# A fused pre-norm attention and SwiGLU block on one core: 38 more of its transposes made by VectorE and a DRAM round trip, in a new list order

## The chip, the cores and the metric

One core of a Trainium2 chip. The metric is device microseconds per execution, the median of the runs. The profile is of one execution; its span goes from the first to the last instruction, and the execution's own time is a little longer. TensorE (PE) runs the matmuls, and in the profile its weight loads stand in a row of their own (PEld); VectorE is DVE, ScalarE is ACT, GpSimd is POOL; every DMA is issued on SyncE's queue (SP), in order.

## What is computed

A sequence of 2048 rows with 640 columns, in float32:

```python
h  = x + A(layernorm(x))        # A: qkv, attention over a window, times wo
h2 = h + B(layernorm(h))        # B: (silu(x @ w_gate) * (x @ w_up)) @ w_down
# A: 32 heads of 20; row s attends to rows s, s-2, ..., s-14 (8 keys, dilated by 2)
# wqkv 640 x 1920, wo 640 x 640, w_gate and w_up 640 x 1728, w_down 1728 x 640
```

## The kernel before

**Tiles.** The rows are cut into four blocks (b = 0 to 3) of 512 rows, each of four tiles j of 128 rows; the 32 heads into four head groups g of 160 columns. Matmuls run on fp32r operands that are split into a high and a low half (a copy by ScalarE, then a `tensor_sub` by VectorE), with three products for each: high times high, high times low, low times high. A block's normalised rows must be turned into columns for TensorE: 20 blocks of 128 x 128 (four row tiles, five column chunks). Their split columns lie in `sha` for blocks 0 and 2 and in `shb` for blocks 1 and 3; the columns of every block's second norm go to `shb` (to `ra` for block 3).

**Stages.** For every block: `load_x` and `ln1` (first norm, to columns), `qkv` for each head group (matmuls L546, evictions L551, DMAs of k, q and v to DRAM), attention of the head group on VectorE (L595 and L602 for the logits, L630 and L638 for the values), the output projection `wo` (L793) with the residual and the second norm, `ln2_columns`, then the FFN (`proj` L863, `down` L874). Blocks 2 and 3 share FFN products (L958, L980). TensorE has QKV and the transposes of block 1 to work on until wo(0), and QKV once more until the first FFN.

**Two ways to turn a norm into columns.** (1) On TensorE: four transposes by a 128 x 128 identity into a PSUM bank, then ScalarE copies the bank as the high half and VectorE subtracts for the low half (`to_columns`, L439, L442, L443; used by `x_columns`). (2) Through DRAM: ScalarE writes the centred or normalised rows sorted by 32 columns into `XN` (`LnStats.one` with `turned`, L300 to L304; `sorted_row`), VectorE turns all 32 x 32 blocks in one instruction (`turn_rows`, L412), four DMAs write to a DRAM tensor (L414 to `ysc`), one DMA reads it back into `XN` as columns (`turned_back`, L420), and ScalarE and VectorE split it (`turned_columns`, L428, L429). `turn_pair` (L381, L383, L387) and `pair_columns` (L395, L396, transposes L404) do that for the first two tiles of a block and leave ten transposes on TensorE for the other two; its DRAM tensor is `zsc`.

The attention's output has the same two ways. In `turned_out` VectorE turns a head group's output (L668) and four DMAs write it to `osc` (L672), from where `wo` loads it as columns. For a block in `TURNED`, the last head group stays in SBUF (`last_rows`, L644) and TensorE transposes it in `last_columns` (L733: per pair of tiles four transposes, one run).

Who goes which way stands at the top of the file (L28 to L30):

```python
TURNED = (0, 3)
HALF = (1, 2)
TURN1 = (2, 3)
```

`TURN1` are the blocks whose first norm goes through DRAM, `HALF` those of which half the second norm does, `TURNED` those whose last head group is transposed on TensorE. Block 1's first norm has its statistics on VectorE (`one_dve`, L347 to L349); block 0's first norm has code of its own in `ln1` (L507).

**The order of the work.** Every piece is added to a `Plan` with an engine, a cost in microseconds, the regions that it reads and writes, and a priority `PR[...]`; from the regions `add` makes its dependencies. `order` runs a list schedule over the engines with these costs: an engine that is free takes the ready piece of the lowest priority number. The start times found, plus hand-set offsets for a few pieces by number (`SHIFT`), are the keys by which all pieces are put into one list; the instructions are emitted in this order, so each engine's queue, SP's too, is a part of it. The semaphores follow from the regions and not from the modelled times.

Of the kernel before, what the change touches and what calls it, by code (L numbers as in the profile page):

```python
# [23 lines left out]
NF = 14  # L24
# [3 lines left out]
TURNED = (0, 3)  # L28
HALF = (1, 2)
TURN1 = (2, 3)  # L30
# [4 lines left out]
LAT, LAT0, RATE = 4.0, 2.0, 350e3  # L35
PR = {'x': 0.5, 'yst': 8, 'yld': 2, 'wqd': 4, 'wqh': 0.5, 'wql': 4, 'qev': 1, 'kvs': 0.4, 'atl': 1.2, 'exp': 0.5, 'ost': 3, 'wod': 2, 'woh': 8, 'wol': 1.2, 'old': 1.5, 'fld': 4, 'lst': 6, 'wev': 1.5, 'fh': 2.2, 'fl': 8, 'ln1': 8, 't1': 1, 'wo0': 1.2, 'wo': 2.2, 'ln1t': 1.2, 'xb': 0.4, 'tr': 10, 't1t': 2.2, 'ln1d': 0.5, 'hst': 10, 'hld': 10, 'ht': 1, 'hc': 2, 'jd': 3, 'jp': 8, 'js': 4, 'jl': 0.4, 'ja': 0.5, 'jfld': 1.2, 'jfh': 4, 'jfl': 1, 'jhi': 4, 'jmu': 0.4, 'jlo': 0.9, 'jcm': 0.5, 'w3': 1, 'w3e': 8, 'w3o': 0.4, 'w3x': 8, 'w3l': 2.2, 'jy': 6}

SHIFT = {
    10: 0.9, 12: 2.5, 34: 4.5, 47: -27.4, 113: 0.8, 131: -5.8, 2096: 10.8, 2101: 6.1, 2156: 4.1, 2712: 6.9,
    2713: 6.6, 2733: -78.6  # L40
# [3 lines left out]
class Plan:  # L44
# [23 lines left out]
    def order(self):  # L68
        ops = self.ops
        left = [len(o[3]) for o in ops]  # L70
        succ = [[] for _ in ops]
        for n, o in enumerate(ops):
            for d in o[3]:
                succ[d].append(n)
# [7 lines left out]
        bus, loaded, start = 0.0, None, [0.0] * len(ops)  # L82
        todo = len(ops)
        while todo:
            best = None
            for e in pend:
                if ready[e]:
                    t = free[e]
                elif pend[e]:
                    t = max(free[e], pend[e][0][0])  # L90
                else:
                    continue
                if best is None or t < best[0]:
                    best = (t, e)
            t, e = best
            while pend[e] and pend[e][0][0] <= t:
                m = heapq.heappop(pend[e])[1]
                heapq.heappush(ready[e], (ops[m][4], m))
            prio, n = ready[e][0]
            if e == "PE" and prio >= 10:  # L100
                soon = min((a for a, m in pend[e] if ops[m][4] == PR["wo0"]), default=1e9)
                if soon < t + 0.3:
                    free[e] = soon
                    continue
            if prio >= 20:
                soon = min((a for a, m in pend[e] if ops[m][4] <= 1), default=1e9)
                if soon < t + ops[n][1] - 0.3:
                    free[e] = soon
                    continue
            heapq.heappop(ready[e])  # L110
            todo -= 1
            _, cost, _, _, _, table, nbytes = ops[n]
            if table is not None and table != loaded:
                cost, loaded = cost + 1.3, table
            start[n] = t
            free[e] = t + cost
            end = t + cost
            if e == "SP":
                bus = max(bus, end) + nbytes / RATE
                free[e] = max(free[e], bus - 3.0)  # L120
                end = bus + (LAT0 if ops[n][4] == 0 else LAT)
            for m in succ[n]:
                same = ops[m][0] == e and e != "SP"
                avail[m] = max(avail[m], end + (0.0 if same else 0.2))
# [3 lines left out]
        self.end = max(free.values())  # L128
        self.start = start
        left = [len(o[3]) for o in ops]  # L130
        key = [(t + SHIFT.get(n, 0.0), n) for n, t in enumerate(start)]
        heap, out = [key[n] for n in range(len(ops)) if not left[n]], []
        heapq.heapify(heap)
        while heap:
            n = heapq.heappop(heap)[1]
            out.append(n)
            for m in succ[n]:
                left[m] -= 1
                if not left[m]:
                    heapq.heappush(heap, key[m])  # L140
        return out
# [9 lines left out]
def nb(chunks, size):  # L151
    return (chunks / 16 * 0.042 + chunks * size / 435e3) * RATE


def act(n):
    return 0.155 + 0.00087 * n


def program(tc, x_in, wqkv_in, wo_in, ffn_in, ffl_in, const_in, out):
# [7 lines left out]
    with tc.tile_pool(name="sb", bufs=1) as sb, tc.tile_pool(  # L167
# [106 lines left out]
        for nm, t in (("K", ksc), ("V", vsc)):  # L274
            P.add(
                "SP", 0.07, lambda t=t: zero_halo(t), r=[rf(PROD, 1120)],
                w=[(f"{nm}{g}{a}", 0, 7) for g in range(NG) for a in range(2)], prio=6, nbytes=36e3,
            )
# [111 lines left out]
        def pair_columns(b):  # L390
# [7 lines left out]
            for u, (n0, n) in enumerate(((10, 4), (14, 4), (18, 2))):  # L398
                bk = (7, 6, 5)[u]
                o, m = 128 * n0, 128 * n  # L400

                def tr(n0=n0, n=n, bk=bk):
                    for q in range(n):
                        T.transpose(banks[bk][:, 128 * q : 128 * q + 128], f(XN + 128 * (n0 + q), 128), ident)  # L404
                P.add("PE", 0.115 * n, tr, r=[rf(XN + o, m), rf(IDENT, 128)], w=[pb(bk)], prio=1)
# [30 lines left out]
        def to_columns(u, src, srcr, dst, dstr, bk, prio):  # L436
# [3 lines left out]
            P.add("PE", 0.46, tr, r=[srcr(4 * u + q) for q in range(4)] + [rf(IDENT, 128)], w=[pb(bk)], prio=prio)  # L440
# [32 lines left out]
        def ln1(b):  # L473
# [3 lines left out]
            st = LnStats(b, src, srcr, 1 if b == 0 else PR["ln1t" if b in TURN1 else "ln1"], rs=RS1 + 4 * b, center=True, turned=b in TURN1)  # L477
            if b:
                if b == 1:
                    st.prio = PR["ln1d"]  # L480
                    for j in range(NJ):
                        st.one_dve(j)
                else:
                    for j in range(NJ):
                        st.one(j)
                st.prio = 2
                st.rstd(0, NJ)
                if b in TURN1:
                    turn_rows(ysc, "Y", b, PR["tr"], PR["yst"])
                    return  # L490
                x_columns(
                    lambda u: (t()[:, 512 * u : 512 * u + 512], t()[:, 2560 + 512 * u : 3072 + 512 * u]),
                    lambda u: ((nm, 512 * u, 512 * u + 512), (nm, 2560 + 512 * u, 3072 + 512 * u)), PR["t1"])
                return
            for j in range(NJ):
# [3 lines left out]
                for c0, n, bk, bo in ((0, 4, 7 - j % 2, 0), (4, 1, 5, j)):  # L499
# [8 lines left out]
                    P.add("PE", 0.115 * n, tr, r=[rf(XN + x0, 128 * n), rf(IDENT, 128)], w=[key], prio=1)  # L508
# [17 lines left out]
        def qkv(b, g):  # L526
# [7 lines left out]
            for j in range(NJ):  # L534
# [12 lines left out]
                for ps in [[x] for x in whole] if b == g == 0 else [whole]:  # L547
                    P.add("PE", 0.218 * len(ps), lambda ps=ps, mm=mm: mm(ps),
# [157 lines left out]
        def last_columns(b, jp, at, sorted_, prio, rot):  # L706
# [27 lines left out]
            P.add("PE", 0.46, tr, r=[rf(last_rows(b, 2 * jp + jj), 160) for jj in range(2)] + [rf(IDENT, 128)], w=[pb(bk)], prio=prio)  # L734
# [6 lines left out]
        def wo(b, prio, bks):  # L741
# [25 lines left out]
            for j in range(NJ):  # L767
# [17 lines left out]
                for half in range(2):  # L785
# [8 lines left out]
                    P.add("PE", 2.25, mm, r=[rr(ot(5 * jp + i), 512) for i in range(5)] + [rr(WO, 6400)], w=[pb(bk)], prio=prio)  # L794
# [21 lines left out]
                if b in (0, 3) and j >= NJ - 2:  # L816
# [43 lines left out]
        def proj(bk, gu, col, wid):  # L860
# [3 lines left out]
            for p, (w, a) in enumerate(((0, 0), (0, 1), (1, 0))):  # L864
                P.add("PE", 1.145, lambda p=p, w=w, a=a: mm(p, w, a), r=[rr(gu + 1280 * w, wid * NC), ("shb", 2560 * a, 2560 * a + 2560)], w=[pb(bk)], prio=10)
# [13 lines left out]
        def downs(batch, first, last, db=DB, cut=False, whole=False):  # L879

            for k in (4, 0, 1, 2, 3):
# [8 lines left out]
                P.add("PE", sum(3 if t[0] < NF - 1 else 2 for t in batch) * 0.229,  # L890
# [61 lines left out]
        def product(bk, terms, start, stop):  # L952

            for p, (w, a) in enumerate(((0, 0), (0, 1), (1, 0))):
# [6 lines left out]
                P.add("PE", 0.229 * n, mm, r=[z for ws, _, cs, xr in terms for z in [rr(ws[w], 256 * len(cs) - 128)] + xr(a)], w=[pb(bk)], prio=10)  # L961
# [7 lines left out]
        def plain(i, x, xr):  # L969
# [6 lines left out]
            for bk, col in ((5, 0), (6, 128))[: 2 if i < NF - 1 else 1]:  # L976
                for p, (w, a) in enumerate(((0, 0), (0, 1), (1, 0))):
# [3 lines left out]
                    P.add("PE", 1.145, mm, r=[rr(gu + 1280 * w, wid * NC)] + xr(a), w=[pb(bk)], prio=10)  # L981
# [171 lines left out]
        def finish(b, db=DB, store=True, final=False):  # L1153
# [7 lines left out]
            P.add("PE", 0.46, tr, r=[rf(so, 512), rf(IDENT, 128)], w=[pb(d4)], prio=0)  # L1161
# [49 lines left out]
        for b, g in first + last:  # L1211
            if g == 0 and b > 0:
# [116 lines left out]
```

## Time and profile before

| | |
|---|---|
| median of 3 runs | 844.8 us (844.69 to 845.16) |
| the profiled execution | 845.0 us, span 843.0 us, granted TensorE clock 1.000 |
| VectorE, busy in the span | 705.1 us (84%) |
| ScalarE, busy in the span | 406.5 us (48%) |
| DMA | 191.12 MB, mean 227 GB/s |

A line of the page's groups or of its chain names the source line (L546 is line 546 of the kernel), engine, operation and tiles, `out<-in`. A row of the timeline begins with the start and the length in microseconds, and ends with the number of instructions merged into it; a bracket behind it tells how long the engine was idle before and which instruction ended that. Matmuls overlap by their pipelining, so a merged row is a little longer than the distance to the next row. A row of the waits says who waited for whom: microseconds in total, times, longest. A row of the DMA issues ends with the count, the size of each and the median time from issue to landing.

### The profile page before, as it was taken

The numbers are of one execution on the slowest core, as the hardware profiler recorded it, in microseconds if no ns is written. First come the engines' busy times: TensorE is split into PE (matmuls) and PEld (weight loads), VectorE is DVE, ScalarE is ACT, GpSimd is POOL, SyncE is SP. The second block draws the span as 40 slices with busy tenths as digits, with TensorE's granted clock in tenths as the row PEclk, the third lists the DMA queues.
The fourth block names the chain that finished last, engine by engine and source line by source line (L and its number), as shares of the span: only waits on it lengthen the run. The fifth ranks groups of instructions, "written<-read, shape, count | busy, mean of one in ns | idle before, by whom it ended". The sixth has DMA issues, their size and how long they took to land.

```text
span 843.0 us, 10782 instructions
## 1 busy us (share of the span) xinstructions
PE 837.8 (99%) x3961; PEld 712.0 (84%) x3961; DVE 705.1 (84%) x841; ACT 406.5 (48%) x674; POOL 24.8 (3%) x33
## 2 busy tenths in 40 slices
PE   9999999999999999999999999999999999999998
PEld 7888888889888888888888898888888888888886
DVE  8899899999998999999999999899434996655552
ACT  6662462344663433775434467456447543333331
POOL 0000000000000100010000010000000000000000
PEclk9999999999999999999999999999999999999999
DMA  8886487467488779468987975888833554444432
GB/s 288 327 314 237 145 272 268 137 209 236 153 290 304 242 257 332 164 207 279 338 329 242 342 242 165 262 329 286 307 111 104 193 177 157 154 169 144 154 113 89
DMA packets 90260, 191.12 MB, mean 227 GB/s; under 512 B 31568, under 2 KB 50896, under 8 KB 89568
## 3 DMA queue, kind: packets, MB, share of 16 engines
q1 hardware_dynamic: 90208, 190.44, 65.7%
q8 instruction: 31, 0.51, 0.2%
q14 instruction: 21, 0.17, 0.1%
HBM read 144.26 MB, written 46.14 MB: 226 GB/s over the span
## 4 chain that ended last, share of the span: by engine, by line
PE 99%; ACT 0%; POOL 0%; DVE 0%; issue 0%; POOLq 0%
PE bank L546 25%; PE bank L874 22%; PE bank L863 22%; PE bank L958 18%; PE bank L793 8%; PE bank L980 2%; PE bank L439 1%; PE bank L454 1%; PE bank L507 0%; PE bank L404 0%; PE bank L1160 0%; PE bank L733 0%; ACT sha L509 0%; POOL ra L1194 0%; DVE h L1168 0%
## 5 line engine op out<-in xcount | busy, mean ns | idle before, releaser
L863 PE MATMUL bank<-shb,ra 128*128 128x512 f32 x810 | 190.2, 390 | 0.0
L863 PEld LDWEIGHTS bank<-shb,ra 128*128 128x128 f32 x810 | 151.4, 188 | 31.4 <-DVE shb L443 0.3
L874 PE MATMUL bank<-ra,acts 128*128 128x512 f32 (+1 forms) x662 | 162.8, 389 | 0.0
L874 PEld LDWEIGHTS bank<-ra,acts 128*128 128x128 f32 x662 | 122.5, 188 | 24.6
L546 PE MATMUL bank<-ra,sha 128*128 128x480 f32 x480 | 105.9, 380 | 0.3 <-ACT sha L509 0.3
L546 PE MATMUL bank<-ra,shb 128*128 128x480 f32 x470 | 102.8, 378 | 0.0
L546 PEld LDWEIGHTS bank<-ra,sha 128*128 128x128 f32 x480 | 89.6, 188 | 14.1 <-ACT sha L509 0.6
L546 PEld LDWEIGHTS bank<-ra,shb 128*128 128x128 f32 x470 | 88.0, 188 | 13.2
L630 DVE TENSOR_TENSOR fa<-fa 128x2560 f32<-128x2560 f32 x32 | 90.3, 2822 | 0.8
L595 DVE TENSOR_TENSOR fa<-fa 128x2560 f32<-128x2560 f32 x32 | 90.2, 2820 | 0.4
L602 DVE TENSOR_REDUCE fa<-fa 128x128 f32<-128x2560 f32 x32 | 89.9, 2810 | 0.5
L551 ACT ACTIVATE st<-bank,fa 128x480 f32<-128x480 f32 x64 | 42.2, 661 | 95.5 <-PE bank L546 87.0
L958 PE MATMUL bank<-shb,ra 128*128 128x512 f32 x360 | 88.0, 391 | 0.0
L958 PEld LDWEIGHTS bank<-shb,ra 128*128 128x128 f32 x360 | 67.1, 188 | 13.5
L638 DVE TENSOR_TENSOR fa<-fa 128x1280 f32<-128x1280 f32 (+2 forms) x68 | 75.9, 1115 | 1.5
L1096 DVE TENSOR_TENSOR fa<-bank,fa 128x512 f32<-128x512 f32 x60 | 41.0, 690 | 42.1 <-PE bank L958 41.1
L793 PE MATMUL bank<-ra 128*128 128x320 f32 x480 | 74.6, 309 | 0.0
L793 PEld LDWEIGHTS bank<-ra 128*128 128x128 f32 x480 | 72.3, 188 | 2.2 <-DVE ra L711 0.2
L958 PE MATMUL bank<-ra 128*128 128x512 f32 x288 | 68.4, 390 | 0.0
L958 PEld LDWEIGHTS bank<-ra 128*128 128x128 f32 x288 | 53.9, 188 | 11.7 <-ACT shb L1017 0.4
L840 ACT CAST ra<-fa 128x1280 fp32r<-128x1280 f32 (+1 forms) x38 | 45.9, 1207 | 28.2 <-PE bank L863 21.4
L908 ACT CAST acts<-fa 128x512 fp32r<-128x512 f32 x47 | 29.1, 620 | 50.7 <-DVE fa L898 25.5
(152 smaller groups left out, 843.7 us busy)
## 6 DMA issues: line engine op xcount, KB each, us to landing
fa<-in_ffn_dram SPq DMA_DIRECT2D x46, 960.0 KB, 6.6
ra<-lsc SPq DMA_DIRECT2D x45, 320.0 KB, 3.4
fa<-ksc SPq DMA_DIRECT2D x16, 880.0 KB, 5.6
fa<-vsc SPq DMA_DIRECT2D x16, 880.0 KB, 6.9
ra<-lsc SPq DMA_DIRECT2D x21, 640.0 KB, 5.3
lsc<-ra SPq DMA_DIRECT2D x13, 640.0 KB, 5.8
ksc<-st SPq DMA_DIRECT2D x16, 320.0 KB, 2.6
qsc<-st SPq DMA_DIRECT2D x16, 320.0 KB, 2.7
```

Source lines behind the costliest of these rows:

```text
L546: T.matmul(banks[bk][:, 0:480], l, r_(wq(g, w, c), 480), start=(p, c) == first_mm, stop=(p, c) == last_mm)
L551: P.add("ACT", act(480) + 0.06, lambda bk=bk, j=j: A.activation(stage_t()[:, so : so + 1920].rearrange("p (t j c) -> p t j c", t=3, j=NJ)[ ...
L595: P.add("DVE", dve(2560), lambda: V.tensor_tensor(f(PROD, 2560).rearrange("p (j w c) -> p j w c", j=2, w=W), window(ko, 2 * jp), f(qo + 32 ...
L602: P.add("DVE", dve(2560), lambda: V.tensor_reduce(f(lo + 128 * jp, 128), f(PROD, 2560).rearrange("p (n d) -> p n d", d=DH), axis=AX.X, op= ...
L630: V.tensor_tensor(f(PROD, 2560).rearrange("p (j w d) -> p j w d", j=2, d=DH), bass.AP(tensor=fa[:, vo : vo + 160].tensor, offset=fa[:, vo ...
L638: V.tensor_add(dst(v), v[:, :, 0:m, :], v[:, :, m : 2 * m, :])
L793: T.matmul(banks[bk][:, 0:320], l, r_(m, 320), start=p == 0 and c == 0, stop=p == 2 and c == NC - 1)
L840: P.add("ACT", act(n), lambda: A.copy(r_(gu, n), f(raw, n)), r=[rf(raw, n)], w=[rr(gu, n)], prio=PR["fh"])
L863: T.matmul(banks[bk], r_(gu + 1280 * w + wid * c + col, 128), x2(a, c), start=p == 0 and c == 0, stop=p == 2 and c == NC - 1)
L874: T.matmul(banks[bk][:, lo:hi], l, m, start=first and p == 0, stop=last and p == len(passes) - 1)
L958: T.matmul(banks[bk], r_(ws[w] + 256 * q, 128), x(a, c), start=start and p == n == q == 0, stop=stop and p == 2 and n == len(terms) - 1 an ...
L1096: dv(0, lambda: V.tensor_add(fb(h, dst), banks[bk], fb(h, src)), [pb(bk)] + fr(h, src), fr(h, dst))
```

## The change

Three settings at the top, and what follows from them:

- `TURN1 = (1, 2, 3)`: block 1's first norm goes through DRAM too (20 transposes). `ln1(1)` now calls `st.one` for its statistics (ScalarE) and `turn_rows`; behind it stand `turned_back` and `turned_columns` for block 1, and only then `load_x(2)` and `ln1(2)`. All of block 1's pieces have the new priority `y1` = 0.6.
- `HALF = (0, 1, 2)`: the first two tiles of block 0's second norm go through `turn_pair` and `pair_columns` (10 transposes); the other two keep ten.
- `TURNED = (3,)`: block 0's last head group goes through `turned_out` and `osc` as the other groups do (8 transposes).

The planner is replaced. Its first pass is the old list schedule with refined costs (gaps between instructions of an engine, at most eight DMAs under way, a DMA's time by chunks and bytes). Then come five rounds: `latest` goes back through the dependencies and finds for every piece the latest time at which it must start if TensorE is to run without a gap in the order found so far; the next list schedule takes the ready piece with the earliest such time. The final keys are the last start times plus a new `SHIFT` with offsets for 49 pieces. No instruction's own work is changed by it, only the order; the costs given to `P.add` are model figures.

```diff
-TURNED = (0, 3)
-HALF = (1, 2)
-TURN1 = (2, 3)
+TURNED = (3,)
+HALF = (0, 1, 2)
+TURN1 = (1, 2, 3)
...
+LANES, HOP = 8, 0.035
+LAP = {"PE": 0.0, "ACT": 0.1, "DVE": 0.08, "POOL": 0.0, "SP": 0.0}
+ROUNDS = ((1.3, 20, 2.5), (1.2, 3, 1.5), (1.1, 3, 3.5), (1.5, 3, 2.5), (1.3, 10, 5.0),)
...
     def order(self):
+        start = self.listed()
+        for stretch, serial, dma in ROUNDS:
+            start = self.listed(self.latest(start, stretch, dma), serial)
...
+        key = [(t + SHIFT.get(n, 0.0), n) for n, t in enumerate(start)]
...
+    def latest(self, start, stretch, dma):
+        ops = self.ops
+        t, due = 5.0, {}
+        for n in sorted((n for n, o in enumerate(ops) if o[0] == "PE"), key=lambda n: start[n]):
+            due[n] = t
+            t += ops[n][1]
+        last = [0.0] * len(ops)
+        for n in reversed(range(len(ops))):
+            eng, cost, _, _, prio, _, nbytes = ops[n]
+            if eng == "SP":
+                cost += nbytes + dma
+            elif eng == "DVE" and prio == 20:
+                cost *= stretch
+            last[n] = min(min((last[m] - HOP for m in self.succ[n]), default=1e9) - cost, due.get(n, 1e9))
+        return last
...
+                heapq.heappush(ready[e], (ops[m][4] if last is None else last[m], m))
...
-            st = LnStats(b, src, srcr, 1 if b == 0 else PR["ln1t" if b in TURN1 else "ln1"], rs=RS1 + 4 * b, center=True, turned=b in TURN1)
+            st = LnStats(b, src, srcr, 1 if b == 0 else PR["y1" if b == 1 else "ln1t"], rs=RS1 + 4 * b, center=True, turned=b in TURN1)
             if b:
-                if b == 1:
-                    st.prio = PR["ln1d"]
-                    for j in range(NJ):
-                        st.one_dve(j)
-                else:
-                    for j in range(NJ):
-                        st.one(j)
+                for j in range(NJ):
+                    st.one(j)
                 st.prio = 2
                 st.rstd(0, NJ)
-                if b in TURN1:
-                    turn_rows(ysc, "Y", b, PR["tr"], PR["yst"])
-                    return
-                x_columns(
...
+                if b:
+                    turn_rows(ysc, "Y", b, *((PR["y1"],) * 2 if b == 1 else (PR["tr"], PR["yst"])))
                 return
...
-                if b in (0, 3) and j >= NJ - 2:
+                if b == 3 and j >= NJ - 2:
...
                     load_x(b)
                     ln1(b)
+                    turned_back(ysc, "Y", b, PR["y1"])
+                    turned_columns(*xt(b), PR["y1"])
                     load_x(2)
                     ln1(2)
```

More of the change, by code (lines that the diff above doesn't have):

```diff
@@ L68, in order, with listed @@
     def order(self):
+        start = self.listed()
+        for stretch, serial, dma in ROUNDS:
+            start = self.listed(self.latest(start, stretch, dma), serial)
+        self.start, self.end = start, max(t + o[1] for t, o in zip(start, self.ops))
         ops = self.ops
         left = [len(o[3]) for o in ops]
[L71 to L74, printed above, removed]
+        key = [(t + SHIFT.get(n, 0.0), n) for n, t in enumerate(start)]
+        heap, out = [key[n] for n in range(len(ops)) if not left[n]], []
+        heapq.heapify(heap)
+        while heap:
+            n = heapq.heappop(heap)[1]
+            out.append(n)
+            for m in self.succ[n]:
+                left[m] -= 1
+                if not left[m]:
+                    heapq.heappush(heap, key[m])
+        return out
+    def latest(self, start, stretch, dma):
[13 more added lines that the diff above has]
+        return last
+    def listed(self, last=None, serial=0.0):
+        ops = self.ops
+        left = [len(o[3]) for o in ops]
+        if last is None:
+            self.succ = [[] for _ in ops]
+            for n, o in enumerate(ops):
+                for d in o[3]:
+                    self.succ[d].append(n)
+        succ = self.succ
         avail = [0.0] * len(ops)
@@ L82, in order @@
         bus, loaded, start = 0.0, None, [0.0] * len(ops)
+        lanes, before, done = [0.0] * LANES, None, [0.0] * len(ops)
         todo = len(ops)
@@ L97, in order @@
                 m = heapq.heappop(pend[e])[1]
[L98 to L110, printed above, removed]
+                heapq.heappush(ready[e], (ops[m][4] if last is None else last[m], m))
+            if last is None:
+                prio, n = ready[e][0]
+                if e == "PE" and prio >= 10:
+                    soon = min((a for a, m in pend[e] if ops[m][4] == PR["wo0"]), default=1e9)
+                    if soon < t + 0.3:
+                        free[e] = soon
+                        continue
+                if prio >= 20:
+                    soon = min((a for a, m in pend[e] if ops[m][4] <= 1), default=1e9)
+                    if soon < t + ops[n][1] - 0.3:
+                        free[e] = soon
+                        continue
+            if e == "DVE" and before is not None:
+                n = min(ready[e], key=lambda x: (x[0] + serial * (before in ops[x[1]][3]), x))[1]
+                ready[e].remove((ops[n][4] if last is None else last[n], n))
+                heapq.heapify(ready[e])
+                if before in ops[n][3]:
+                    t = max(t, done[before] + HOP)
+            else:
+                n = heapq.heappop(ready[e])[1]
             todo -= 1
@@ L113, in order @@
             if table is not None and table != loaded:
-                cost, loaded = cost + 1.3, table
+                t, loaded = t + 1.3, table
             start[n] = t
-            free[e] = t + cost
-            end = t + cost
+            free[e] = t + cost - LAP[e]
+            end = done[n] = t + cost + (0.06 if e == "PE" else 0.0)
             if e == "SP":
-                bus = max(bus, end) + nbytes / RATE
-                free[e] = max(free[e], bus - 3.0)
-                end = bus + (LAT0 if ops[n][4] == 0 else LAT)
+                bus = max(bus, end + 0.6) + nbytes
+                end = done[n] = bus + 1.6
+                lanes.append(end)
+                free[e] = max(free[e], lanes[-LANES])
+            elif e == "DVE":
+                before = n
             for m in succ[n]:
                 same = ops[m][0] == e and e != "SP"
-                avail[m] = max(avail[m], end + (0.0 if same else 0.2))
+                avail[m] = max(avail[m], free[e] if same else end + HOP)
                 left[m] -= 1
@@ L127, in order @@
                     heapq.heappush(pend[ops[m][0]], (avail[m], m))
[L128 to L141, printed above, removed]
+        return start
 def dve(n):
```

35 lines of the change are left out of this document (15 added, 20 removed), and 6 rows, old and new, of the table SHIFT.

## The prediction

> **What bounds the kernel now.** I read the page's first part, then its chain, then the waits of TensorE alone, then TensorE's timeline. The first fence holds the page's span, its busy times and the chain's shares by engine; the second is the whole answer on what TensorE (PE) waited for: microseconds in total, times, longest.
>
> ```profile
> span 843.0 us, 10782 instructions
> PE 837.8 (99%) x3961; PEld 712.0 (84%) x3961; DVE 705.1 (84%) x841; ACT 406.5 (48%) x674; POOL 24.8 (3%) x33
> ...
> PE 99%; ACT 0%; POOL 0%; DVE 0%; issue 0%; POOLq 0%
> ```
>
> ```profile
> PE bank L454 <- POOL ra L1194: 1.3, 1, 1.3
> PE bank L546 <- ACT sha L509: 0.3, 1, 0.3
> ```
>
> TensorE has two waits in the whole span, both at its start. But a busy PE is not proof: a matmul's end is modelled, so I look at the starts. The timeline of PE (start, length, group) in the middle of the first FFN:
>
> ```profile
> 298.04 6.96 PE L863 MATMUL bank<-shb,ra 128*128 128x512 f32 x30
> 304.84 0.84 PE L874 MATMUL bank<-acts,ra 128*128 128x512 f32 x3
> 305.52 2.88 PE L874 MATMUL bank<-ra,acts 128*128 128x512 f32 x12
> 308.24 6.96 PE L863 MATMUL bank<-shb,ra 128*128 128x512 f32 x30
> ```
>
> 45 matmuls take 308.24 - 298.04 = 10.20 us, 227 ns each, start to start. The kernel is the length of TensorE's list: what leaves the list shortens the kernel, and what other engines do costs nothing until it makes PE wait. [...]
>
> **The change part by part: what leaves TensorE.** Second block's first norm (ln1(1)): 20 transposes go, in runs of 12 and 8 among the QKV matmuls (L546).
>
> ```profile
> 29.13 1.47 PE L439 MATMUL bank<-fa 128*128 128x128 f32 x12
> 30.36 3.49 PE L546 MATMUL bank<-ra,sha 128*128 128x480 f32 x15
> 33.69 1.04 PE L439 MATMUL bank<-fa 128*128 128x128 f32 x8
> 34.48 29.42 PE L546 MATMUL bank<-ra,sha 128*128 128x480 f32 x135
> 63.74 52.00 PE L546 MATMUL bank<-ra,shb 128*128 128x480 f32 x240
> 115.58 24.78 PE L546 MATMUL bank<-ra,sha 128*128 128x480 f32 x114
> ```
>
> An undisturbed QKV matmul costs (115.58 - 63.74)/240 = 0.216 us. From 29.13 to 34.48 are 5.35 us, of which 15 x 0.216 = 3.24 are matmuls: 2.11 for the transposes. The 135 matmuls behind them take 29.26 instead of 29.16, 0.10 more: going back from transposes costs about 0.1 once. So **2.2 us** go.
>
> First block's second norm (ln2(0)): today 20 transposes in the same two runs, then ten.
>
> ```profile
> 231.35 1.03 PE L439 MATMUL bank<-fa 128*128 128x128 f32 x8
> 232.15 3.49 PE L546 MATMUL bank<-ra,shb 128*128 128x480 f32 x15
> ...
> 236.70 1.32 PE L546 MATMUL bank<-ra 128*128 128x480 f32 x5
> ```
>
> 236.70 - 231.35 - 3.24 + 0.1 = 2.2 us. The half that stays is the code that block 1 runs now, in two runs of four and one of two; its first run of four:
>
> ```profile
> 374.29 0.60 PE L404 MATMUL bank<-fa 128*128 128x128 f32 x4
> 374.64 3.02 PE L874 MATMUL bank<-ra,acts 128*128 128x512 f32 x12
> ```
>
> 0.35 and the 0.1 behind it make 0.45 for four, so ten of them cost about 1.1 us and **1.1 us** go. The first block's last head group (L733) loses two runs of four, the first of which is:
>
> ```profile
> 160.94 0.60 PE L733 MATMUL bank<-fa 128*32 128x128 f32 x4
> 161.30 19.69 PE L546 MATMUL bank<-ra,shb 128*128 128x480 f32 x90
> ```
>
> 0.36 + 0.1, twice: **0.9 us**. Sum: 2.2 + 1.1 + 0.9 = 4.2 us.
>
> **What is added elsewhere.** The norm of block 1 leaves VectorE's bn_stats for ScalarE's sums, as blocks 2 and 3 have them. VectorE's rows (the statistics of one of four row tiles, which it loses, then a block transpose as it gets one), and ScalarE's first and last row instruction of block 2:
>
> ```profile
> 22.72 0.88 DVE L347 BATCH_NORM_STATS2 fa<-fa 128x6 f32<-128x320 f32 x2
> ...
> 48.83 2.85 DVE L412 STREAM_TRANSPOSE fa<-fa 128x2560 f32<-128x2560 f32 x1 [0.62 <-ACT fa L302]
> ```
>
> ```profile
> 38.57 0.73 ACT L300 ACTIVATE fa<-fa 128x640 f32<-128x640 f32 x1
> ...
> 47.97 0.83 ACT L302 ACTIVATE fa<-fa 128x640 f32<-128x640 f32 x1
> ```
>
> VectorE loses 4 x 0.88 = 3.5 us in the statistics alone, and the subtractions behind them, and gets 2.85 there; for ln2(0) it gets half a block transpose, an estimated 1.4, and for the head group the small ones, while small sums and splits go. All in all it does about as much as before. ScalarE gets 10.2 us of rows (38.57 to 48.80, with what stands between them) and some 4 of squares, at 48% busy. SP gets about 16 issues more: five each through ysc and zsc, eight osc writes against two loads fewer, some 10 us in an order that nothing can overtake. All this I cost at nothing, since PE has QKV or FFN matmuls to run meanwhile; if that cover ends, every microsecond counts in full. GpSimd's work stays as it is, though DMAs of the head groups around it move.
>
> **The new list order** moves instructions of every engine. Its own cost has no row. Downwards it is bounded by PE's waits, 1.6 us in all; upwards by the two waits priced below. I take 0, because the order of before holds PE without a gap for all but these waits, with the same buffers and mostly the same chains; the ends go into the range. The two places where chains get tighter:
>
> Place one, block 1's columns. PE has only block 0's QKV until 63.74, in future until 63.74 - 2.2 = 61.5. The rows of the round trip: median issue to landing, the last three writes of block 2 on SP, and the splits of block 3 on ScalarE and VectorE.
>
> ```profile
> ysc<-fa SPq DMA_DIRECT2D x8, 320.0 KB, 4.9
> fa<-ysc SPq DMA_DIRECT2D x2, 1280.0 KB, 7.9
> ```
>
> ```profile
> 66.50 2.66 SPq L414 DMA_DIRECT2D ysc<-fa  x3
> ```
>
> ```profile
> 148.80 2.69 ACT L428 CAST shb<-fa 128x512 fp32r<-128x512 f32 x5
> ```
>
> ```profile
> 149.68 3.09 DVE L429 TENSOR_TENSOR shb<-fa,shb 128x512 fp32r<-128x512 f32 x5
> ```
>
> The input is there by 22.7 (L347 starts without a wait). Rows 10.2, block transpose 2.85, four writes issued in about 3, landing 4.9, load 7.9, columns 152.77 - 148.80 = 4.0: done at 55.6. 5.9 us to spare.
>
> Place two, the first FFN's start. All 4.2 us lie ahead of it, so its input must come 4.2 us earlier.
>
> ```profile
> 240.02 13.98 PE L863 MATMUL bank<-shb,ra 128*128 128x512 f32 x60
> ```
>
> ```profile
> 232.08 2.83 DVE L595 TENSOR_TENSOR fa<-fa 128x2560 f32<-128x2560 f32 x1
> ...
> 240.17 1.25 DVE L443 TENSOR_TENSOR shb<-bank,shb 128x512 fp32r<-128x512 f32 x2
> ```
>
> ```profile
> 327.96 2.36 PE L793 MATMUL bank<-ra 128*128 128x320 f32 x15
> ```
>
> The last low halves are written until 241.42, and the pass that reads them comes five matmuls (1.13 us) after 240.02: nothing to spare. But VectorE does an attention product of block 1 (L595) right before, whose use is the output projection at 327.96. An order that puts such work (2.8 us a piece) behind the norm's chain makes up the 4.2 us, and half of the columns no longer wait for TensorE.
>
> **Sum.** The profiled execution took 845.0 us with a span of 843.0, and the median of the three runs is 0.2 lower. Span 843.0 - 4.2 = 838.8, plus 2.0 around it 840.8, less 0.2: **840.6 us**.
>
> **The rivals.** *The first FFN does not start earlier.* If the chain ahead of 240 us stays where it is, PE waits there for what it saved: 844.8. For it: the chain has no slack and VectorE is the fuller of the helpers. Against it: the attention work that can step back, and fewer columns at the end. A part of it, 1 to 3 us lost here or at the later hand-overs, would give 842 to 844.
>
> *Block 1's columns come late (slower).* SP issues in order, and block 2's writes show what that can do: its rows were done at 48.80 and the last write was issued at 69.16. With landing 4.9, load 7.9 and columns 4.0 that is 37.2 us behind the rows. Block 1's rows are done at 33.0 at the earliest, so at this pace the columns come at 70.2, 8.7 us after 61.5, and nothing else is ready for PE: 840.6 + 8.7 = 849.3. It costs from 5.9 us of delay on and turns the change into a loss from 10.1 on. For it: the rows just quoted, and that ScalarE also owes the casts of the QKV weights at that time. Against it: block 2 had no hurry, its columns were used at 115.58 only. [...] No run here shows what follows for a hurried round trip, so the chance stays small.
>
> *The order gains at the start* what PE waits now, up to 1.6 us: 839.0. *The transposes stay on PE*: 844.8; the code gives no reason.
>
> **How the numbers follow.** A run tells about 0.2% (1.7 us) from no change: faster is below 843.1, slower above 846.5. Full gain, 839.8 to 841.8: 0.67. Better than that: 0.03. A part lost, 841.8 to 844.5: 0.11, of it 0.08 faster and 0.03 same. FFN not earlier or transposes kept: 0.07, same. Block 1 late: 0.12, slower. So faster 0.78, same 0.10, slower 0.12. The range 839.6 to 845.0 leaves out the late columns and the better half of the start's gain, under 2 in 10.
>
> **What would show it.** MATMULs fall from 3961 to 3923: 40 transposes of L439 go, 8 of L733, and L404 gets 10. PE's waits stay near 2 us. QKV on shb starts near 61.5 without a wait, the first FFN near 236. A PE wait on a split of shb at about 60 us, or at 236 on VectorE, proves one of the two rivals; a PE wait elsewhere of over 2 us would make the zero for the new order wrong.

## The result

The changed kernel takes **852.8 us** (median of 5 runs, 852.28 to 854.67) where the kernel before takes 844.8 beside it: 1.0099 of its time, 95% interval 1.0084 to 1.0113. The change makes the kernel 1% slower; 840.6 was forecast, and the range ended at 845.0. The profiled execution took 852.3 us, with a span of 850.1.

The new code stands some lines further down: the QKV matmuls L546 are L580 now, their evictions L551 are L585, the FFN's L863 and L874 are L897 and L908, and its casts into `acts`, L908, are L942. The page after, its first part, the row of the granted clock in 40 slices, and the chain:

```profile
span 850.1 us, 10764 instructions
PE 836.3 (98%) x3923; PEld 708.0 (83%) x3923; DVE 692.7 (81%) x826; ACT 417.1 (49%) x700; POOL 23.7 (3%) x33
...
PEclk9999999999998999999999999999999999999999
...
PE 79%; DVE 12%; DMA 3%; issue 2%; ACT 2%; SPq 1%; DVEq 0%; ACTq 0%
```

The 38 matmuls are gone (3961 to 3923), and TensorE is busy 1.5 us less, in a span that is 7.1 us longer. VectorE's busy time fell by 12.4 us. The chain says what changed in kind: of before it was TensorE to 99%, now other engines, DMAs and issuing own a fifth of it. All that TensorE waited for:

```profile
PE bank L908 <- ACT acts L942: 4.4, 1, 4.4
PE bank L992 <- DMA ra<-lsc: 1.4, 1, 1.4
PE bank L541 <- DVE sha L544: 1.3, 1, 1.3
PE bank L497 <- POOL ra L1228: 1.3, 1, 1.3
PE bank L541 <- DVE fa L392: 1.3, 2, 0.7
PE bank L992 <- DVE fa L1130: 0.3, 1, 0.3
```

The waits are 8.4 us longer than before (10.0 against 1.6) and the list should be 4.2 us shorter; that doesn't give 7.1. So I took TensorE's starts: for each line the ordinary distance from one start to the next (0.216 us for QKV, 0.227 for the FFN, and so on) times its count, and apart from that all that the starts lie further from each other.

| us | before | after | |
|---|---|---|---|
| ordinary distances, all matmuls | 835.3 | 831.2 | -4.1 |
| beyond them: to 20 us (the start) | 1.5 | 2.65 | +1.1 |
| 220 to 260 us | 0.2 | 7.4 | +7.2 |
| 540 to 580 us | 0.2 | 2.1 | +1.9 |
| all other places together | 0.7 | 1.35 | +0.7 |
| from TensorE's last matmul to the end | 3.5 | 3.8 | +0.3 |

The sum is +7.1, the whole difference of the spans. (In no row are 1.6 us that both spans have, most of them the 1.3 us ahead of TensorE's first matmul. With medians by line as the ordinary distances the rows come out within 0.2 us of these.) The list did get 4.1 us shorter; one place, at 250 us, took 7.2 and used that up.

**The place.** The timelines of the changed kernel there, TensorE first, then ScalarE, SP and GpSimd:

```profile
237.72 13.34 PE L897 MATMUL bank<-shb,ra 128*128 128x512 f32 x58
255.42 1.95 PE L908 MATMUL bank<-acts,ra 128*128 128x512 f32 x3 [4.36 <-ACT acts L942]
257.17 4.35 PE L908 MATMUL bank<-ra,acts 128*128 128x512 f32 x12
```

```profile
247.69 0.60 ACT L931 ACTIVATE fa<-bank 128x512 f32<-128x512 f32 x1 [3.27 <-PE bank L897]
248.19 0.66 ACT L585 ACTIVATE st<-bank,fa 128x480 f32<-128x480 f32 x1
254.75 0.62 ACT L942 CAST acts<-fa 128x512 fp32r<-128x512 f32 x1 [5.90 <-DMA osc<-fa]
```

```profile
249.77 0.78 SPq L591 DMA_DIRECT2D ksc<-st  x1
250.60 0.60 SPq L599 DMA_DIRECT2D qsc<-st  x1
251.25 0.57 SPq L591 DMA_DIRECT2D vsc<-st  x1
```

```profile
254.97 0.10 POOL L1274 MEMSET acts<- 128x2 f32 x1 [20.17 <-DMA osc<-fa]
```

Read from the bottom: `acts`, the FFN's activations, and `st`, the stage for q, k and v, are one buffer at two times (both have the tag `ab`). `acts` can be written only when the last QKV's rows have been evicted into `st` (ScalarE, L585, 248.19) and stored by three DMAs (issued 249.77 to 251.82). So the first cast into `acts` starts at 254.75, and TensorE's first `down` waits 4.36 us. (The profile names `osc`, whose writes are issued right behind the three stores; the buffer's rule concerns the stores.) The same steps of before, on ScalarE and on GpSimd:

```profile
240.22 0.67 ACT L551 ACTIVATE st<-bank,fa 128x480 f32<-128x480 f32 x1 [2.44 <-PE bank L546]
...
248.78 0.62 ACT L908 CAST acts<-fa 128x512 fp32r<-128x512 f32 x1 [0.69 <-ACT ra L840]
```

```profile
245.59 0.10 POOL L1238 MEMSET acts<- 128x2 f32 x1 [8.84 <-DMA vsc<-st]
```

There the last eviction was 8 us earlier, and the buffer was free at 245.6, 3.2 us ahead of its first use. In the changed kernel one piece of the plan, number 419 (the eviction of QKV for block 3, head group 3, tile 2), has the offset `419: 18.3` in `SHIFT`: it is put behind the second silu of the FFN.

**The second loss at the place.** The 12 matmuls behind the wait take 257.17 to 261.35, 4.18 us instead of 12 x 0.227 = 2.72, and the three ahead of them 1.75 instead of 0.68. The windows (start:end, length, PE busy, granted clock, DMA share, GB/s) tell why:

```profile
250.00:253.41 3.41, 1.06 (x5) 1.00 0.99 381
253.41:256.83 3.42, 1.41 (x3) 0.50 0.25 67
256.83:260.24 3.41, 3.41 (x10) 0.50 0.64 191
260.24:263.65 3.41, 3.41 (x17) 1.00 0.78 241
```

The granted clock is 0.50 from 253.41, during the wait, to 260.24, which is 6.83 us, and 1.00 behind that. So TensorE works at half its clock for the first 4.8 us behind the wait: 2.5 us more. In the 3.41 us ahead of 253.41 TensorE was busy for 1.06 (the last section has what followed other waits).

**The two places that the prediction looked at have no long wait.** QKV on block 1's columns starts without one, 3.1 us after VectorE has written the last of them (59.61), and the first FFN came 2.8 us earlier than before (240.02):

```profile
56.51 3.10 DVE L472 TENSOR_TENSOR shb<-fa,shb 128x512 fp32r<-128x512 f32 x5 [0.91 <-ACT shb L471]
```

```profile
62.71 12.48 PE L580 MATMUL bank<-ra,shb 128*128 128x480 f32 x57
...
237.18 3.00 PE L897 MATMUL bank<-shb,ra 128*128 128x512 f32 x12
```

Ahead of that FFN, VectorE still does an attention product and a reduction between the norm's statistics (228.95) and its last columns (239.36):

```profile
229.88 2.82 DVE L629 TENSOR_TENSOR fa<-fa 128x2560 f32<-128x2560 f32 x1
...
233.28 2.81 DVE L636 TENSOR_REDUCE fa<-fa 128x128 f32<-128x2560 f32 x1
```

### The profile page after: what moved, and what is told of

The parts are those of the page before. It is cut to its first block, busy times and chain, and to the rows that moved or that the text cites. A ratio compares the mean times of both kernels' runs of the same rounds, so it can differ in the third digit from the quotient of the medians.

```text
span 850.1 us, 10764 instructions
## 1 busy us (share of the span) xinstructions
PE 836.3 (98%) x3923; PEld 708.0 (83%) x3923; DVE 692.7 (81%) x826; ACT 417.1 (49%) x700; POOL 23.7 (3%) x33
## 4 chain that ended last, share of the span: by engine, by line
PE 79%; DVE 12%; DMA 3%; issue 2%; ACT 2%; SPq 1%; DVEq 0%; ACTq 0%
PE bank L580 19%; PE bank L908 19%; PE bank L992 17%; PE bank L897 16%; PE bank L827 6%; DVE fa L636 2%; DVE fa L664 2%; DVE fa L629 2%; DVE fa L672 2%; PE bank L1014 1%; DMA ra<-lsc 1%; DMA fa<-in_x_dram 1%; DMA zsc<-fa 1%; DVE ra L891 1%; DVE fa L932 0%
## 5 line engine op out<-in xcount | busy, mean ns | idle before, releaser
L897 PE MATMUL bank<-shb,ra 128*128 128x512 f32 x810 | 189.9, 390 | 0.0
L897 PEld LDWEIGHTS bank<-shb,ra 128*128 128x128 f32 x810 | 151.5, 188 | 31.5 <-ACT ra L874 0.4
L908 PE MATMUL bank<-ra,acts 128*128 128x512 f32 (+1 forms) x662 | 162.9, 392 | 0.0
L908 PEld LDWEIGHTS bank<-ra,acts 128*128 128x128 f32 x662 | 124.0, 190 | 25.4
L580 PE MATMUL bank<-ra,sha 128*128 128x480 f32 x480 | 104.8, 379 | 0.0
L580 PE MATMUL bank<-ra,shb 128*128 128x480 f32 x470 | 102.5, 378 | 0.0
L580 PEld LDWEIGHTS bank<-ra,sha 128*128 128x128 f32 x480 | 89.8, 188 | 13.6
L580 PEld LDWEIGHTS bank<-ra,shb 128*128 128x128 f32 x470 | 88.1, 188 | 13.2
L629 DVE TENSOR_TENSOR fa<-fa 128x2560 f32<-128x2560 f32 x32 | 90.2, 2817 | 0.4
L636 DVE TENSOR_REDUCE fa<-fa 128x128 f32<-128x2560 f32 x32 | 90.1, 2814 | 0.3
L585 ACT ACTIVATE st<-bank,fa 128x480 f32<-128x480 f32 x64 | 41.9, 657 | 56.4 <-PE bank L580 51.3
L992 PEld LDWEIGHTS bank<-ra 128*128 128x128 f32 x288 | 54.1, 188 | 11.2
L942 ACT CAST acts<-fa 128x512 fp32r<-128x512 f32 x47 | 29.1, 619 | 64.1 <-DVE fa L932 42.7
L874 ACT CAST ra<-fa 128x1280 fp32r<-128x1280 f32 (+1 forms) x38 | 45.8, 1204 | 24.3 <-PE bank L897 15.4
```

The costliest lines, as they stand in the source:

```text
L580: T.matmul(banks[bk][:, 0:480], l, r_(wq(g, w, c), 480), start=(p, c) == first_mm, stop=(p, c) == last_mm)
L585: P.add("ACT", act(480) + 0.06, lambda bk=bk, j=j: A.activation(stage_t()[:, so : so + 1920].rearrange("p (t j c) -> p t j c", t=3, j=NJ)[ ...
L629: P.add("DVE", dve(2560), lambda: V.tensor_tensor(f(PROD, 2560).rearrange("p (j w c) -> p j w c", j=2, w=W), window(ko, 2 * jp), f(qo + 32 ...
L636: P.add("DVE", dve(2560), lambda: V.tensor_reduce(f(lo + 128 * jp, 128), f(PROD, 2560).rearrange("p (n d) -> p n d", d=DH), axis=AX.X, op= ...
L874: P.add("ACT", act(n), lambda: A.copy(r_(gu, n), f(raw, n)), r=[rf(raw, n)], w=[rr(gu, n)], prio=PR["fh"])
L897: T.matmul(banks[bk], r_(gu + 1280 * w + wid * c + col, 128), x2(a, c), start=p == 0 and c == 0, stop=p == 2 and c == NC - 1)
```

## The experiments

Theory: the transposes do gain 4.1 us; the loss is made by the list order, most of it by the one late eviction. Rivals: the moved parts' own chains through DRAM make the loss; or the order as a whole does. In every group the times of before are of the same chip (844.8 to 845.0 in the four groups).

### The eviction put back

**e1_no_419**, the changed kernel without that offset:

```diff
-    ... 419: 18.3, ...
```

> The changed kernel without the one offset of 18.3 us on the eviction of the last head group's third row tile. Theory (the late eviction keeps the stage buffer from the FFN's first gate): PE's wait of 4.4 us at 251 us and the 2.9 us of matmuls at half speed behind it go, 852.8 - 7.4 = 845.4 us. Rival (the DMAs in front of the buffer are late because of the added round trips): the wait stays and the time is 852 to 853 us.

848.0 us, 1.0041 (1.0026 to 1.0056): 4.8 us come back. The wait of 4.4 us and the half clock are gone (the mean granted clock is 1.0), but another wait is there, `PE bank L447 <- ACT fa L420: 1.6, 1, 1.6`: the eviction now stands ahead of the norm's rows (L420) in ScalarE's list and waits itself for its matmuls:

```profile
232.80 0.66 ACT L585 ACTIVATE st<-bank,fa 128x480 f32<-128x480 f32 x1 [0.80 <-PE bank L580]
233.36 1.72 ACT L420 ACTIVATE fa<-h,fa 128x640 f32<-128x640 f32 x2
```

So some offset had a purpose; 18.3 was too much.

**e5_419_by_3**, the eviction just behind those rows:

```diff
-    ... 419: 18.3, ...
+    ... 419: 3, ...
```

> The changed kernel with the late eviction's offset at 3 us instead of 18.3, which puts it right behind the second norm's last rows and ahead of the splits. Theory (with no offset it stood ahead of those rows, waited for its QKV matmuls and held them up by 1.6 us; with 18.3 it came too late for the stage buffer): neither wait, so 1.6 to 2 us under the run without the offset, 846 us. Rival (any place of it costs as much): 848 us or more.

846.5 us, 1.0019 (1.0009 to 1.0028): 6.3 us of the 8.0 come back with one number. TensorE at the place has no wait for the buffer, which GpSimd's timeline now shows free at 244.44:

```profile
237.59 13.86 PE L897 MATMUL bank<-shb,ra 128*128 128x512 f32 x60 [0.27 <-DVE shb L450]
251.29 0.84 PE L908 MATMUL bank<-acts,ra 128*128 128x512 f32 x3
251.97 2.88 PE L908 MATMUL bank<-ra,acts 128*128 128x512 f32 x12
```

```profile
244.44 0.10 POOL L1274 MEMSET acts<- 128x2 f32 x1 [9.23 <-DMA vsc<-st]
```

### The same eviction made late in the old kernel

**e3_before_late_eviction**: the kernel before, none of whose transposes is moved, with its number for the same piece:

```diff
+    414: 18.3,
```

> The kernel before, with the eviction of that same tile 18.3 us later in the list and nothing else. Theory: the same wait and the same slow matmuls arise without any transpose moved, 844.8 + 7.4 = 852.2 us. Rival (the added round trips make the wait): no wait, 844.8 us.

855.0 us, 1.0118 (1.0103 to 1.0133). The mechanism stands without any of the change's transposes, and costs 10.0 us here, more than in the changed kernel: the stores keep the cast waiting for 8.55 us (the profile names `vsc`, the third), TensorE waits 7.0 us, and the matmuls behind it are slow again, at 0.50 of the clock from 260.8 to 263.8. ScalarE's timeline, then TensorE's:

```profile
251.00 0.66 ACT L551 ACTIVATE st<-bank,fa 128x480 f32<-128x480 f32 x1
260.20 0.62 ACT L908 CAST acts<-fa 128x512 fp32r<-128x512 f32 x1 [8.55 <-DMA vsc<-st]
```

```profile
260.87 1.95 PE L874 MATMUL bank<-acts,ra 128*128 128x512 f32 x3 [7.01 <-ACT acts L908]
```

### Order and settings apart

**e2_no_offsets**: the changed kernel with `SHIFT = {}`.

> The changed kernel without any hand-set offset. Theory: the wait at 251 us goes, as without the one offset; what the other 48 offsets gain or cost is not known, 841 to 849 us. Rival (the new planner's own order keeps PE waiting there): a wait of several us stays at 251 us, 850 us or more.

861.3 us, 1.0186 (1.0168 to 1.0204). 841 to 849 was expected: a miss. There is no wait for the stage buffer, but there are others, the longest 3.5 us at 216 us. The new planner alone is not a good order; the other 48 offsets are worth about 13 us (861.3 against 848.0).

**e9_new_order_old_settings**: the new planner, no offsets, `TURNED`, `HALF`, `TURN1` and the code behind them as before.

> The new planner without any hand-set offset, on the old settings: the order alone, to be held against the new settings without offsets (861.3 us). If 38 transposes less are worth their 4.2 us and the new order covers the round trips, 865 us; if the round trips cost more than they save, less than 861 us; and above 845 us the new planner's raw order is weaker than the old one with its offsets.

863.2 us, 1.0215 (1.0188 to 1.0243). Against e2 this is the three moved parts under one and the same planner: they gain 1.9 us of their 4.1, and the two intervals overlap. Against before, the planner without offsets costs 18.

**e4_settings_alone**: the old planner and its 12 offsets (renumbered), with the three moved parts.

> The three settings and their code alone, in the order of the old planner with its twelve offsets. Theory (38 transposes less are worth their 4.2 us wherever the order covers the round trips): 840.6 to 845 us, with 3923 matmuls. Rival (block 1's columns come late, or the first FFN starts no earlier): PE waits at 61 us or 236 us, 845 to 850 us.

907.4 us, 1.0738 (1.072 to 1.0756), far above both expectations. Under the old order block 1's columns come 12.3 us late at 61 us (31.7 - 19.4), and block 3's and others behind them too. From its waits of TensorE:

```profile
PE bank L537 <- ACT shb L428: 31.7, 2, 19.4
PE bank L404 <- ACT fa L377: 5.5, 1, 5.5
```

**e7_first_norm_alone**: the old planner, of the three only `TURN1 = (1, 2, 3)`.

> The old planner with its offsets, and of the three settings block 1's first norm alone through DRAM. Theory (most of the 62 us that the three settings cost in the old order come from the first norms' round trips, block 1's and those queued behind it): PE waits near 61 and 171 us, 880 to 895 us. Rival (the second norm's half makes them): 845 to 860 us.

883.6 us, 1.046 (1.0439 to 1.0481): `PE bank L537 <- ACT shb L428: 23.6, 2, 12.6`. The shorter of the two waits is the slower rival of the prediction, at 61 us; with the same settings the new order has no such wait.

The two parts that aren't hurried, in the old order with its offsets (renumbered), together and alone:

```diff
-TURNED = (0, 3)
-HALF = (1, 2)
+TURNED = (3,)
+HALF = (0, 1, 2)
...
-                if b in (0, 3) and j >= NJ - 2:
+                if b == 3 and j >= NJ - 2:
```

**e13_two_small_parts** has all of it, **e15_head_group_alone** only `TURNED`, **e16_half_norm_alone** only the rest.

> The kernel before with its own list order and offsets (renumbered), and two of the three parts: half of the first block's second norm and one head group turned through DRAM, 18 transposes; the second block's first norm stays as it was, so block 1's columns are not hurried. Theory (a transpose that leaves TensorE's list is worth its pitch, 1.1 and 0.9 us, as long as the list keeps the other engines ahead): 842.9 us, 0.998 of before. Rival (the chain into the first FFN, at 232 to 240 us, has no slack, so what is saved is waited for there, or the order makes a new wait of its own): 844.8 us or above, with a wait of TensorE in the trace that before does not have.

> The kernel before, its own order, with one head group turned through DRAM and nothing else: 8 transposes leave TensorE. Theory: 0.9 us gained, 844.0 us, with the first FFN starting as late as before if the norm's chain has no slack, and then 844.8. Rival (the eight small writes of osc and the loads behind them hold SP's queue, and the output projection of block 0 waits): 845 to 848 us, with a wait on the columns of the attention.

> The kernel before, its own order, with half of the first block's second norm turned through zsc and nothing else: 10 transposes leave TensorE just ahead of the first FFN. Theory: 1.1 us gained, 843.7 us. Rival (the norm's chain through DRAM is longer than through TensorE, and the first FFN waits for it): 845 to 849 us, with a wait on shb near 236 us.

863.7 us (1.0222, 1.0208 to 1.0236), 856.3 (1.0135, 1.0122 to 1.0149) and 852.4 (1.0094, 1.008 to 1.0108). All three wait for the first FFN's norm, each for 5 us or more. First e15's largest wait; then e16's timelines of SP, with the load that its columns need, of ScalarE and of TensorE:

```profile
PE bank L439 <- ACT fa L377: 7.1, 2, 6.9
```

```profile
230.56 0.61 SPq L387 DMA_DIRECT2D fa<-zsc  x1
```

```profile
243.43 1.63 ACT L395 CAST shb<-fa 128x256 fp32r<-128x256 f32 x5
```

```profile
243.88 8.43 PE L863 MATMUL bank<-shb,ra 128*128 128x512 f32 x23 [5.17 <-ACT shb L395]
```

In e16 the load is issued at 230.56 and takes 10.3 us to land, at about 240.9: already later than the 238.7 at which TensorE was free. The other 2.5 us are ScalarE's list, which puts casts of weights and an exponential with its table load (1.28 us) ahead of the columns. In the mended new order (e6 below) the same load is issued 6.5 us earlier (SP's timeline), and the wait for it is gone:

```profile
224.01 0.38 SPq L430 DMA_DIRECT2D fa<-zsc  x1
```

So each of the three parts costs more than it saves when it is put into the old order: net losses of 7.5, 11.4 and 38.7 us. Under the new planner without offsets the three together cost nothing measurable (e2 against e9). I had expected 842.9 to 844.0 us for these last three: a miss, the parts have no gain of their own in the old order.

### Can the rest be had?

**e6_stores_later**: e5, and three output stores of block 1 later in the list, behind which SP issues the load of `lsc` that TensorE waits for at 577 us (issued at 568.33, right behind the stores).

```diff
+    1780: 30, 1784: 30, 1786: 30,
```

> As the run before, and three output stores of block 1 30 us later on SP's queue. Theory (they stand ahead of the loads of the FFN's low halves, for which PE waits 1.5 us at about 572 us): that wait goes, 1.5 us less than the run before, 844.5 us. Rival (the loads are late by their own length): no gain.

845.9 us, 1.0007 (0.9997 to 1.0016), level with before. That wait is gone, but 844.5 was expected: a miss, as e5's own trace has only 0.4 us left of it. Against e5 the medians differ by 0.6 us, with overlapping intervals. What is left of TensorE's waits:

```profile
PE bank L497 <- POOL ra L1228: 1.3, 1, 1.3
PE bank L827 <- ACT fa L830: 0.9, 1, 0.9
PE bank L541 <- DVE sha L544: 0.9, 1, 0.9
```

Beside these there are a few of 0.3 us and less. The starts beyond the ordinary distances add up to 7.25 us, 4.7 more than before, in five places of about 1 us (the start, 232 to 238, 322, 567 to 572, 620 to 700). That eats what the list saves.

**e10_start_as_before** (e6, the start's instructions keyed as of before), **e11_four_offsets** (e6, with these offsets) and **e12_start_and_offsets** (both) go for these places:

```diff
+    AT = {0: 0.0, 1: 0.4, ...}   # key of the pieces of the first 17 us
...
-    ... 999: 2.1, 1001: 4.8, 1007: 5, ... 2732: 67.5, ...
+    ... 624: 4.5, 1034: -3, ...
```

> The changed kernel with 419 at 3, the three stores 30 us later in the list, and the instructions of the first 17 us listed in the order that they have in the kernel before. Theory (what is left of the loss is made of short waits that the new list order brings, those of L541 at the start being the first): these waits of 1.3 and 1.3 us fall to the one of some 1.3 us that the kernel before has, and the time comes to about 845.0 us, 0.9 us below the 845.89 us of the run without this edit. Rival (the start is set by what the first loads and VectorE deliver, whatever the list): the time stays at 845.9 us, the waits move to other lines of the first 20 us.

> The changed kernel with 419 at 3, the three stores later, and four more edits of the offsets: instruction 1034 3 us earlier (the eviction for which L827 waits 0.9 us at 322), 624 4.5 us later (a wait of L897 of 0.3 us at 237), the offsets of 999, 1001 and 1007 and of 2732 taken out (the tail after TensorE's end is 0.33 us longer with them). Theory: each of the three losses goes, 1.5 us together, to about 844.4 us. Rival (the offsets were fitted to this order and hold other waits away): the waits named go but others of 1 to 2 us come, and the time is 845.5 to 848 us.

> Both edits together: the start's order of the kernel before, and the four edits of offsets. Theory (the transposes taken off are worth 4.2 us and only short waits of the list eat them): the gains add, 0.9 and 1.5 us below 845.89, to about 843.5 us, below the kernel before by 0.2%. Rival (each wait removed brings the next one, as the engines behind TensorE have no room left): 845 to 846 us, no better than the kernel before.

846.3 (1.0016, 1.0007 to 1.0025), 847.3 (1.0032, 1.0019 to 1.0044) and 848.3 (1.0042, 1.0028 to 1.0055): the rival in e10 and e11, and above both expectations in e12. A wait that is removed comes up elsewhere. In e12, whose lines are 14 higher, the first two rows were 0.9 and nothing in e6:

```profile
PE bank L841 <- ACT fa L844: 2.3, 2, 1.7
PE bank L911 <- DVE fa L946: 1.3, 1, 1.3
```

No version beat the kernel before. Whether an order exists that keeps all of the 4.1 us stays open; a few offsets did not find it.

## Why the prediction was wrong

- **The list is the bound, and 4.2 us leave it: right.** TensorE's ordinary distances sum up to 4.1 us less, and 3923 matmuls are left.
- **VectorE does about as much, ScalarE 14 us more: the size was off.** VectorE's busy time fell by 12.4 us (its instructions' own times, which overlap a little, by 5.7 together), ScalarE's rose by 10.6. What that is worth in time isn't shown.
- **Place one, block 1's columns, 5.9 us to spare: no wait, as forecast, but with 3.1 us to spare.** QKV on `shb` starts at 62.71; 61.5 was forecast, and the start's 1.1 us are in between. The columns were done at 59.6 and not at 55.6. Three terms of the sum were off: the input came at 27.4 instead of 22.7 (ScalarE waits 2.74 us for the load of `x`), the rows then took 7.4 us instead of 10.2, and the load from `ysc`, issued at 46.80, took 9.0 instead of 7.9. The slower rival there had a real mechanism: e4 and e7 show it at 12 us, and e4, which has the settings of the changed kernel, that the order decides.
- **Place two, the first FFN: the start nearly right, the way there not.** It starts 2.8 us earlier instead of 4.2, and again 1.1 of the missing 1.4 is lost in the first 20 us. The attention product that was to step back did not: between the norm's statistics and its last columns VectorE still does a product (L629, 229.88) and a reduction (L636, 233.28), as it did before (L595, L602). What the new order moved away is smaller work (low halves of weights, a sum of the values, block transposes): in that stretch VectorE had 9.6 us of other work before and has 6.4 now. e13, e15 and e16 show what the old order makes of this place.
- **The step that failed: the zero for the new list order.** "I take 0, because the order of before holds PE without a gap for all but these waits, with the same buffers and mostly the same chains." That is evidence for the old order, not for a new one: a new order's zero has to be shown place by place. It measured +11.2 us (10.9 at TensorE's starts, 0.3 at the end), of it 6.9 at the shared buffer (4.4 of wait, 2.5 of slow matmuls); the other 4.3 are in shorter waits and gaps, for which no run shows one cause. e5 takes 6.3 us of the time away with one offset, and e3 makes the wait in the old kernel with one. The prediction had named the sign for this: "a PE wait elsewhere of over 2 us would make the zero for the new order wrong". PE's waits were to stay near 2 us; they are 10.0. The upper bound, "the two waits priced below", held for two places only. The hand-over from `st` to `acts`, with 3.2 us to spare of before, was in the profile, as GpSimd's memset at 245.59 against the cast at 248.78; I did not look there, since no transpose went through it. And the offset `419: 18.3` was in the diff, with a sign and a size that can be held against that slack.
- **A wait costs its length ("every microsecond counts in full"): too little for a long one.** 4.4 us cost 6.9, since the granted clock was 0.50 for 4.8 us behind it.

What the document shows: the mechanism of the loss at 250 us (taken away in e5, made in e3), and that moved parts and order need each other (e4, e7, e13, e15, e16, e9 and e2). What it doesn't settle: which of the remaining 1 us places is whose. e10 to e12 removed waits there and got others.

## What to carry to other kernels

When a change replaces the order of a list that keeps the bounding engine full, price every buffer that changes owner, not only the data that the change moves: find its release and its first use in the profile of before, and hold the new offsets against the slack between them. A list kept full by hand-set offsets has none of its gains for free: parts worth 0.9 to 2.2 us each cost 7 to 39 in an order that was not made for them. And price a long wait of TensorE above its length: the 4.4 us of the changed kernel cost 6.9, as the granted clock was 0.50 for 4.8 us behind the wait, and behind the 7.0 us of e3 and the 2.1 us of e9 it was 0.50 as well.

## What the runs showed of the hardware

The half clock also came after waits well under the 4.4 us of the changed kernel. In e9 a wait of 2.14 us ends at 237.31, and ten matmuls follow at twice their distance, at a granted clock of 0.50 to 240.73. In e4 two waits of 1.0 us, both between 269.4 and 272.9, are followed by 0.50 too. e12 waits 1.69 us, until 471.34, and keeps its clock of 1.00. e9's windows, then e4's, then e12's:

```profile
233.91:237.32 3.41, 1.27 (x9) 1.00 0.47 154
237.32:240.73 3.41, 3.41 (x11) 0.50 0.98 399
```

```profile
269.50:272.91 3.41, 1.42 (x8) 1.00 0.51 171
272.91:276.33 3.42, 3.42 (x15) 0.50 0.98 237
```

```profile
469.03:472.45 3.42, 1.73 (x10) 1.00 0.46 184
472.45:475.86 3.41, 3.41 (x20) 1.00 0.00 0
```

So the length of a single wait did not sort these cases: 1.0 us twice was followed by 0.50, and 1.69 us by 1.00. In the 3.41 us ahead of the half clock TensorE was busy for 1.06 us in the changed kernel, for 1.27 in e9 and for 1.42 in e4; ahead of the full clock in e12 for 1.73. Two waits of nearly one length differed as well: behind 1.40 us in e2, until 8.39, the clock was 0.72 in the mean over 8 to 14 us, and behind 1.36 us in the changed kernel, until 577.78, it was 1.00 over 578 to 584. Behind the longer waits it was low: 0.50 from 243.7 to 249.0 behind 6.91 us in e15, and 0.50 from 243.8 to 249.0 behind 5.17 in e16. What sets the clock isn't shown by these runs.
